# A retention and snake-activation kernel on one core: who casts the first half of batch 2, and when the last state sum of batch 1 is added

## The chip, the cores and the metric

The kernel runs on one core of a Trainium2 chip. A core has TensorE (matrix products into PSUM), VectorE (called DVE in the profile), ScalarE (ACT), GpSimd (POOL), SyncE (SP, here used to issue DMAs) and DMA engines. Each engine takes its instructions in the order in which they stand in its own queue, and waits where a semaphore says so. The metric is the device time of one execution in microseconds (us). Before the change it was 311.66 us, the median of three runs (311.43 to 312.88).

## The reference

For every batch (8), head (8), 576 tokens and head size 64, a masked and decaying attention without softmax is computed, its heads are laid side by side as a row of 512, and a two-layer product with a snake activation follows:

```python
scores = scale * np.matmul(q, k.transpose(0, 1, 3, 2))
gamma = 1.0 - 2.0 ** (-5.0 - np.arange(H, dtype=np.float32))
Dmat = np.where(rel >= 0, gamma[:, None, None] ** rel[None, :, :], 0.0)   # rel = row - column
ret = scores * Dmat[None, :, :, :]
attn_out = np.matmul(ret, v)
x = attn_out.transpose(0, 2, 1, 3).reshape(B * S, H * D)                  # 4608 x 512
h = x @ w_in                                                              # 512 -> 2048
s = np.sin(alpha * h)
g = h + s * s / (alpha + 1e-09)
out = g @ w_out                                                           # 2048 -> 512
```

All inputs and the output are 32-bit floats.

## The kernel before

**Attention.** The first 512 tokens of a batch are done in four chunks of 128, two to a half (p = 0, 1); the last 64 tokens of all batches are gathered into a ninth block. Because the decay is a power of gamma, it can be split into a factor on q and one on k: q and k are loaded as 32-bit numbers and multiplied by those factors (table cn) while being cast to 16 bits. This multiplication is the "cast" of this text: step C, function cast_half (line 203). One cast covers half of the heads of one half p of q or of k, 128 partitions by 512 numbers. On VectorE or GpSimd it is one instruction (line 215); on ScalarE it is eight of 128 x 64 (line 210), as there the factor is a value for each partition. Both casts of k and both of q must be there before the 16 transposes of that half (TR, line 275), which TensorE does for batches 0 to 2 half 0 and DMA transposes (CR, line 232) do for the rest. Then come scores (SP, line 376), mask (SM, line 393), values (VA, line 462) and the part that comes from earlier chunks through a state (ST, line 488); the result is copied to x as 16 bits (XT).

**State.** What chunk c hands on is a sum: kvs[c] = kvs[c-1] times gamma to the 128 (FA, "faded", line 330) plus the product of k and v of chunk c, which stands in PSUM (NS, "next sum", line 334, always on VectorE, since the product is in PSUM). TS (line 346) makes the 16-bit state of it. The three steps of the last chunk of batch 1 are FA 1 2, NS 1 3 and TS 1 3; the last state is used by the ninth block at the end.

**PSUM.** There are three tags: mm (two buffers of two banks each), hp (three banks) and op (one). Transposes, scores, the products of k and v and the values all use mm, and a new tile waits until an older one has been read for the last time.

**The two products.** A block n of 512 tokens is one batch. Its first product (G1, line 584) has 16 units of 128 columns, each with a sine (SI), a square (SQ) and a sum with the product (PR, line 609). The second (G2, line 623) makes 128 rows in four parts and copies them out (OS, with two DMAs on SP each).

**Order.** For batches 0 to 2 the order is written out by hand: TABLE (lines 637 to 977), one step to a line, is followed from top to bottom (lines 1144 to 1150) under a manual schedule, so that each engine gets its instructions in the order in which they stand in the table. The last letter of a step is its engine: V VectorE, A ScalarE, G GpSimd. Loads (LK for q and k on SP, LV for v on GpSimd) stand in the same table. From batch 3 on a loop (line 1158) sets the order. The steps around the change are at lines 829 to 872: the end of batch 1's attention, the second product of block 0, the casts and transposes of batch 2's first half, and the first units of block 1.

Of the kernel before, what the change touches and what calls it, by code (L numbers as in the profile page):

```python
# [16 lines left out]
def kernel(  # L17
# [816 lines left out]
G2 0 1 2 hp  # L834
G2 0 1 3 hp
G2 0 2 3 hp
OS 0 1 A
OS 0 2 A
NS 1 2
# [5 lines left out]
ST 1 1  # L845
XT 1 1 A
OS 0 0 A
C 2 q 0 1 V
C 2 k 0 0 V
G2 0 3 3 hp  # L850
C 2 q 0 0 V
C 2 k 0 1 V
TR 2 0 k
TR 2 0 q
TK 2 0 k A
G1 1 0 hp
SI 1 0
FA 1 2 G
NS 1 3
OS 0 3 V  # L860
TS 1 3 G
C 2 k 1 1 G
# [118 lines left out]
    V, A_, G_ = nc.vector, nc.scalar, nc.gpsimd  # L981

    with tc.manual_schedule():
# [174 lines left out]
        for n in range(2, NBLK):  # L1158
            A = A2
# [104 lines left out]
```

## Time and profile before

| what | value |
|---|---|
| median of three runs | 311.66 us |
| the profiled execution | 311.75 us, span 309.8 us |
| busy share of TensorE, VectorE, ScalarE, GpSimd | 96%, 62%, 73%, 43% |
| a cast of line 215 on VectorE, least and median of the q casts | 0.679 and 0.686 us |
| a cast of line 215 on GpSimd, median of the q casts | 1.050 us |
| one of the 16 instructions of line 210 on ScalarE | 0.333 us |
| a state sum of line 334 | 0.408 to 0.422 us |
| a DMA transpose of k or q, issue to landing | 3.1 to 10.0 us |

The profile shows one execution, traced by instruction. Times in it count from the start of the span; the execution's own time is 1.95 us longer than the span. In a timeline a row gives start, duration, engine, line, operation, output and inputs, and in brackets how long the engine had stood idle and who released it. The chain of waits is followed back from the last instruction: each row is what the next one waited for. A name such as q stands for a raw and for a cast tile alike.

### The profile page before, as it was taken

To read this page: it belongs to the slowest core of one execution; us is meant where nothing else is said; L and a number is where in the kernel's file an instruction comes from. 1 tells how busy PE (TensorE), PEld (TensorE's weight loads), DVE (VectorE), ACT (ScalarE), POOL (GpSimd) and SP (SyncE) were. 2 spreads that over 40 slices of the span, in tenths; PEclk is the share of its full clock that TensorE was granted. 3 is DMA by queue.
4 is the path that set the end of the run, shared out by engine and by line. 5 is a ranking of instruction groups with operands and counts; after the bars stand their busy time and mean duration, and the time that the engine had idled before them with its cause. 6 is when DMAs were issued, how large, how long until landed. Compare 5 with 4: busy or idle time off the path is not lost.

```text
span 309.8 us, 7642 instructions
## 1 busy us (share of the span) xinstructions
PE 296.7 (96%) x3145; PEld 152.7 (49%) x3145; DVE 192.2 (62%) x267; ACT 224.9 (73%) x370; POOL 133.8 (43%) x158
## 2 busy tenths in 40 slices
PE   5799989899899999999999999999999999999995
PEld 5586454444444444544454444544544444444444
DVE  2688957799665356965997699655666343444301
ACT  1469961699588887788778878787787888888810
POOL 3878655669969819901980198209100000000000
PEclk9579999999999999999999999999999999999999
DMA  8999999996999787999999989996331111122133
GB/s 217 210 186 198 262 190 291 180 232 133 152 183 233 157 203 179 118 170 221 170 165 190 178 185 195 164 131 96 70 68 37 35 36 34 34 49 54 34 67 68
DMA packets 118017, 44.74 MB, mean 144 GB/s; under 512 B 84432, under 2 KB 113504, under 8 KB 117984
## 3 DMA queue, kind: packets, MB, share of 16 engines
q1 hardware_dynamic: 83792, 35.08, 55.9%
q0 software_dynamic: 33600, 8.92, 29.7%
q8 instruction: 24, 0.39, 0.6%
q10 hardware_dynamic: 592, 0.28, 0.4%
q14 instruction: 9, 0.07, 0.1%
HBM read 36.91 MB, written 9.44 MB: 150 GB/s over the span
## 4 chain that ended last, share of the span: by engine, by line
PE 80%; DVE 8%; DMA 4%; POOL 3%; ACT 2%; issue 1%; SPq 1%; DVEq 0%; POOLq 0%; ACTq 0%
PE ops L623 37%; PE hps L584 32%; DMA qT<-q 2%; DVE ret L393 2%; DMA k<-in_k_dram 2%; DVE gT L609 2%; PE o L462 2%; PE o L488 2%; PE hps L1065 2%; PE sc L376 1%; PE kv L312 1%; PE ops L1226 1%; PE tr L275 1%; PE sc L407 1%; DVE gT L1092 1%; DVE kvs L334 1%
## 5 line engine op out<-in xcount | busy, mean ns | idle before, releaser
L609 DVE SCALAR_TENSOR_TENSOR gT<-ss_t,inva,hps 128x512 f16<-128x512 f16 x136 | 100.6, 745 | 80.3 <-ACT ss_t L602 79.9
L623 PE MATMUL ops<-w_out,gT 128*128 128x512 f16 x560 | 140.8, 379 | 0.0
L584 PE MATMUL hps<-x,w_in 128*128 128x512 f16 x480 | 120.9, 379 | 1.0 <-DVE gT L609 0.7
L593 ACT ACTIVATE s_t<-hps,alpha_t 128x512 f16<-128x512 f32 x136 | 92.8, 685 | 33.2 <-PE hps L584 32.1
L584 PEld LDWEIGHTS <-w_in 128*128 128x128 f16 x544 | 52.8, 98 | 64.6 <-issue 1.6
L623 PEld LDWEIGHTS <-gT 128*128 128x128 f16 x560 | 53.0, 98 | 60.9 <-DVE gT L609 0.3
L602 ACT ACTIVATE ss_t<-s_t 128x512 f16<-128x512 f16 x127 | 79.9, 631 | 2.6
L346 POOL TENSOR_TENSOR s<-kvs,cn 128x512 f16<-128x512 f32 x28 | 30.2, 1078 | 60.0 <-ACT kvs L319 50.9
L633 ACT COPY osb<-ops 128x512 f32<-128x512 f32 x31 | 18.1, 585 | 13.5 <-PE ops L623 13.1
L126 POOL DMA_DIRECT2D v<-in_v_dram x32 | 22.0, 730 | 0.0
L393 DVE TENSOR_TENSOR ret<-sc,mask 128x1024 f16<-128x1024 f32 x12 | 14.4, 1215 | 6.1 <-PE sc L376 6.1
L215 DVE TENSOR_TENSOR q<-q,cn 128x512 f16<-128x512 f32 x18 | 15.4, 880 | 4.2 <-DMA q<-in_q_dram 4.2
L584 PE MATMUL hps<-x_rest,w_in 128*128 128x512 f16 x64 | 16.4, 379 | 0.0
L432 DVE TENSOR_TENSOR ret<-sc,two 128x1024 f16<-128x1024 f32 x12 | 14.6, 1218 | 0.0
L215 POOL TENSOR_TENSOR q<-q,cn 128x512 f16<-128x512 f32 x14 | 14.6, 1054 | 0.1
L236 ACT CAST x<-o 128x1024 f16<-128x1024 f32 (+1 forms) x13 | 10.8, 851 | 3.7 <-PE o L488 3.4
L604 POOL TENSOR_TENSOR ss_t<-s_t 128x512 f16<-128x512 f16 x10 | 10.4, 1056 | 6.4 <-ACT s_t L593 4.0
L359 POOL TENSOR_TENSOR kvs<-s,kvs 128x256 f32<-128x256 f32 x15 | 11.5, 769 | 1.2
L358 POOL TENSOR_TENSOR s<-kvs,cn 128x256 f32<-128x256 f32 x15 | 11.0, 730 | 0.0
L215 POOL TENSOR_TENSOR k<-k,cn 128x512 f16<-128x512 f32 x9 | 9.9, 1109 | 0.8 <-DMA k<-in_k_dram 0.7
L462 PE MATMUL o<-ret,v 64*64 64x128 f16 (+1 forms) x512 | 10.1, 218 | 0.1
L462 PEld LDWEIGHTS <-v 64*64 64x64 f16 x512 | 7.6, 110 | 4.8 <-issue 4.3
(73 smaller groups left out, 208.1 us busy)
## 6 DMA issues: line engine op xcount, KB each, us to landing
out_dram<-osb SPq DMA_DIRECT2D x70, 128.0 KB, 2.5
q<-in_q_dram SPq DMA_DIRECT2D x14, 512.0 KB, 7.0
k<-in_k_dram SPq DMA_DIRECT2D x32, 128.0 KB, 4.6
k<-in_k_dram SPq DMA_DIRECT2D x7, 512.0 KB, 7.4
q<-in_q_dram SPq DMA_DIRECT2D x8, 256.0 KB, 5.1
v<-in_v_dram POOLq DMA_DIRECT2D x8, 256.0 KB, 5.8
w_in<-in_moe_w_in_dram POOLq DMA_DIRECT2D x4, 512.0 KB, 6.9
w_out<-in_moe_w_out_dram POOLq DMA_DIRECT2D x4, 512.0 KB, 8.3
```

The lines of the kernel that those rows point to most:

```text
L126: nc.gpsimd.dma_start(t_[halves(g), :, s], v[b, :, xs, :].rearrange("h i d -> i h d"))
L215: eng.tensor_tensor(half[b, nm, p][:, :, :, t, :], raw[b, nm, p].rearrange("p (a t) (r d) -> p a t r d", t=2, r=2)[:, :, t], (ct if nm == ...
L346: (eng or nc.gpsimd).tensor_tensor(d_, self.kvs[:, n].unsqueeze(2).to_broadcast([P, 4, 2, D]), g2.unsqueeze(3).to_broadcast([P, 4, 2, D]), ...
L393: nc.vector.tensor_tensor(ret.rearrange("p t (z x) -> p (t z) x", z=2)[:, :, 0:n], sc.rearrange("p t (z x) -> p (t z) x", z=2)[:, :, 0:n], ...
L432: nc.vector.tensor_tensor(ret.rearrange("p t (a x) -> p (t a) x", a=n), sc.rearrange("p t (a x) -> p (t a) x", a=n), m_.unsqueeze(1).to_br ...
L462: nc.tensor.matmul(o[g][halves(t), x0 : x0 + 128].rearrange("p (r i) -> p r i", r=2)[:, :, i0:], x, y, start=(t, g) not in begun, stop=las ...
L584: nc.tensor.matmul(hps, w_in16[:, a, fc * P : (fc + 1) * P], x_of[n][:, a], start=(a == 0), stop=(a == KT - 1),)
L593: nc.scalar.activation(s_t, hps, mybir.ActivationFunctionType.Sin, bias=0.0, scale=alpha_t[:, fc : fc + 1],)
L602: nc.scalar.activation(ss_t, s_t, mybir.ActivationFunctionType.Square)
L609: nc.vector.scalar_tensor_tensor(gT[n][:, fc, :], ss_t, inva[:, fc : fc + 1], hps, MULT, ADD)
L623: nc.tensor.matmul(ops[n, c], gT[n][:, fk, c * P : (c + 1) * P], w_out16[:, fk, :], start=(fk == 0), stop=(fk == FC - 1),)
L633: nc.scalar.copy(osb, ops.pop((n, c)))
```

## The change

Four steps of the table move or change engine; no function is changed. The cast of q's half 1 (C 2 q 0 1) goes from VectorE to ScalarE and stands 11 lines higher, ahead of the output copies OS 0 1 and OS 0 2. VectorE's order of k, q, k casts becomes k, k, then the sum NS 1 3 (with its fade FA 1 2 on GpSimd ahead of it in the table), then the remaining q cast. Before, the fade and the sum stood behind the transposes and the first unit of block 1.

```diff
 G2 0 2 3 hp
+C 2 q 0 1 A
 OS 0 1 A
 OS 0 2 A
 NS 1 2
...
 XT 1 1 A
 OS 0 0 A
-C 2 q 0 1 V
 C 2 k 0 0 V
 G2 0 3 3 hp
+C 2 k 0 1 V
+FA 1 2 G
+NS 1 3
 C 2 q 0 0 V
-C 2 k 0 1 V
 TR 2 0 k
 TR 2 0 q
 TK 2 0 k A
 G1 1 0 hp
 SI 1 0
-FA 1 2 G
-NS 1 3
 OS 0 3 V
 TS 1 3 G
 C 2 k 1 1 G
```

## Prediction

> **What bounds the kernel now.** I read the page first (chain that ended last, busy shares), then the chain from 48 to 62 us, then the orders of VectorE, GpSimd, TensorE and ScalarE there, and last the busy time by stage. The stage table, in which the columns after the stretch are its length, PE, PEld, DVE, ACT, POOL (with instruction counts), clock, DMA share and GB/s:
>
> ```profile
> 54.19:56.99 2.80, 1.83 (x29) 1.10 (x28) 2.80 (x7) 1.69 (x3) 0.00 (x0) 1.00 1.41 249
> ...
> 60.17:71.39 11.22, 10.65 (x182) 5.39 (x172) 11.05 (x17) 10.44 (x19) 8.37 (x10) 1.00 0.97 223
> ...
> 83.01:305.90 222.89, 222.88 (x2136) 108.65 (x2136) 130.82 (x166) 169.69 (x267) 76.16 (x94) 1.00 0.78 123
> ```
>
> From 83.01 us TensorE is busy for 222.88 of 222.89 us at clock 1.00: whatever brings its arrival there forward ends the kernel earlier by as much. The change acts at 54 to 57 us, where VectorE is full, TensorE has a gap and GpSimd stands still. The chain of waits there:
>
> ```profile
> 52.75 1.44 DVE ret L393
> 54.19 0.60 DVE q L215
> 54.80 0.60 DVE k L215
> 55.40 0.60 DVE q L215
> 56.00 0.60 DVE k L215
> 56.60 0.34 DVE kvs L334
> 56.95 0.04 issue
> 56.99 1.05 PE tr L275 x16
> ```
>
> Four casts and the state sum (NS 1 3) stand in line on VectorE, and batch 2's transposes start when the sum ends. TensorE's own order shows the gap, GpSimd's and ScalarE's what they do meanwhile:
>
> ```profile
> 55.06 1.03 PE L623 MATMUL ops<-w_out,gT 128*128 128x512 f16 x4
> 56.99 0.61 PE L275 MATMUL tr<-ident,k 128*128 128x128 f16 x8 [0.91 <-DVE kvs L334]
> 57.43 0.61 PE L275 MATMUL tr<-ident,q 128*128 128x128 f16 x8
> 57.88 1.89 PE L584 MATMUL hps<-x,w_in 128*128 128x512 f16 x8
> ```
> ```profile
> 53.02 0.61 POOL L330 TENSOR_TENSOR s<-kvs,cn 128x256 f32<-128x256 f32 x1
> 57.01 1.04 POOL L346 TENSOR_TENSOR s<-kvs,cn 128x512 f16<-128x512 f32 x1 [3.38 <-DVE kvs L334]
> ```
> ```profile
> 52.93 0.58 ACT L236 COPY osb<-ops 128x512 f32<-128x512 f32 x1 [5.96 <-PE ops L623]
> 53.79 0.58 ACT L236 COPY osb<-ops 128x512 f32<-128x512 f32 x1 [0.28 <-PE ops L623]
> 55.26 1.01 ACT L236 CAST x<-o 128x1024 f16<-128x1024 f32 x1 [0.88 <-PE o L488]
> ```
>
> The reader is to see three things. The first transpose waited for the sum, not only for its data: it writes the PSUM buffer from which the sum reads (two buffers carry the tag mm). ScalarE is idle for 5.96 us before 52.93. The sum's other input was ready at 53.02 + 0.61 = 53.63, long before its turn.
>
> **The change, part by part.**
>
> *A q cast leaves VectorE.* One instruction of 0.68 us, 0.60 from start to start, goes off the chain: all that follows it there can start 0.60 sooner.
>
> *It becomes eight instructions on ScalarE.* The 16 of the same kind (line 210) took 3.91 us in all with 0.333 each, so one every (3.91 - 0.333)/15 = 0.238; eight end 7 x 0.238 + 0.333 = 2.0 us after the first starts. They wait for the load of q, issued at 43.81 and landed 6.7 us later, at 50.5, so they end at about 52.5, inside the idle 5.96 us: cost nothing. Behind them stand OS 0 1, OS 0 2, XT 1 1, OS 0 0 and TK 2 0. OS 0 1 starts at 52.93, so 0.4 us is spare; the two copies (about 0.5 each from start to start) are followed by an idle 0.88, so XT 1 1 at 55.26 moves only if the cast ends after 54.26.
>
> In a sentence of its own: the Trainium skill, ScalarE: Activation LUTs, Rules for kernel authors, gives multiplies to VectorE and budgets some 0.3 us per ACTIVATE plus 0.83 ns per element, by which eight of 64 would take an estimated 2.8 us and end at 53.3; OS 0 1 would slip 0.4 us and the sum would stay, since the trace's 0.238 decides.
>
> *The k casts move up, the sum goes ahead of the last q cast.* VectorE becomes k at 54.12, k at 54.72, sum at 55.32 (ends 55.73 instead of 56.94), q at 55.65, ending 56.33. The first k was cast at 54.72 without a wait and would now be asked for at 54.12; its load, issued at 44.37, landed 8.0 us later, at 52.4, so no wait. The fade (FA 1 2) keeps its place in GpSimd's order, as no other GpSimd step lies between its old and new line, and nothing is issued to a DMA queue by any step moved; the order on SP is unchanged.
>
> *TensorE.* G2 0 3 3 starts at 55.06 and passes the array to the next group 4 x 0.217 later, at 55.93. Then sum (55.73) and k casts (55.40) are done: the k transposes run from 55.93 to 56.37. The q transposes need q at 56.33; between a cast's end and the load of its weights lay 0.06 (56.60 to 56.66), between that and the matmul 0.16 to 0.33, so they start between 56.55 and 56.72, say 56.6, and the next product (G1 1 0) 0.45 later, at 57.05 instead of 57.88: 0.83 us gained (0.71 to 0.88). If the transposes got another mm buffer, the one XT 1 1 empties at 56.27, the k part would start at 56.33 and G1 at 57.2: 0.66. I take 0.83, since the trace names the sum as releaser. G1's input from XT 1 1 (56.27) is there.
>
> *GpSimd.* Its to-state (TS 1 3) is released at 55.80 instead of 57.01, but a q cast with two SBUF inputs is running then. The nearest row is at 49.94: VectorE's 0.69 us (line 346) met a GpSimd fade released at 49.98, and the fade took 1.12 instead of 0.61 while VectorE lost nothing. So TS 1 3 ends 0.47 + (1.04 - 0.61) = 0.9 after the cast, at 57.2 instead of 58.05: 0.8 earlier, in step with TensorE. Its four casts for batch 2's second half, ending at 62.08, and the transposes on SP behind them follow; k and q for them land at 54.5 and 56.2, in time.
>
> *Where the gain goes.* From 60.17 VectorE, TensorE and ScalarE hand each other work (11.05, 10.65 and 10.44 of 11.22 us), so all shift. The last wait before the full stretch is TensorE's 0.82 us at 83.01 for batch 3's q transpose by DMA, issued at 75.84 and landed 7.0 us later; its issue hangs on GpSimd's casts, and these on ScalarE's sines, which shift as well. The only fixed things are loads: if batch 3's stayed where they are, q (64.03 + 5.7 = 69.7) would meet a cast moved from 70.23 to 69.4 and take back 0.3.
>
> Sum: -0.60 (cast away) and -0.60 (sum ahead of the other), cut to -0.83 by the q cast and TensorE's own order; all else 0. The profiled execution took 311.75 us (span 309.8 and 1.95 around it), 0.09 above the median: 311.75 - 0.83 = 310.92, against the median 311.66 - 0.83 = 310.8.
>
> **The rivals.**
>
> *GpSimd takes the port first.* If TS 1 3 starts before the q cast, the cast waits. At 39.57 GpSimd had started and VectorE's cast at 40.13 took 1.07 instead of 0.68, ending 0.56 after GpSimd. Then q ends at 55.80 + 1.04 + 0.56 = 57.4, G1 starts at 58.1: 0.2 slower, 311.9. For it: the two come within 0.15 us. Against: VectorE starts its next instruction 0.07 before the one in front ends, GpSimd 0.07 after it. The Trainium skill, SBUF — State Buffer, Who interferes with whom, says the same: an instruction with two SBUF inputs on VectorE and a reading one on GpSimd block each other whole, and issue order decides who waits; by that rule it is all or nothing, and the two rows agree.
>
> *ScalarE waits for q (slower).* Place: the first of the eight. The load lands at 50.5; the slowest of this line's loads in the profile took 10.8 us, which would be 54.6. Then the cast ends at 56.6, XT 1 1 at 58.6, and G1 starts at 58.65: 0.8 slower, 312.4. It decides once q lands after 53.8; from 53.0 on it eats the gain. Against: all that precedes this load is untouched.
>
> *Eaten downstream.* Batch 3's loads do not move, or another stage has slack that fills: 0.3 to 0.8 lost, 311.1 to 311.7.
>
> *Batch 3's DMA transposes move by themselves.* These landed after 3.1 to 10.0 us in this profile, the deciding one after 7.0, in a stretch with DMA share 1.32. At under 6 us TensorE's wait is gone and the gain grows to 0.83 + 0.98 (82.03, when it was free, to 83.01) = 1.8: 309.85. At 10.0 it costs 3.0 - 0.83 = 2.2: 313.8; over 9.4 it decides beyond the bound below. For it: the order of traffic shifts. Against: the loads, the value load and the transposes all hang on the same shifting engines.
>
> **How the numbers follow.** Forecast (0.5 to 1.1 gained) 0.50; eaten downstream 0.13; port 0.07; q late 0.05; DMA transposes sooner 0.13, later 0.12. About 0.5%, 1.56 us, is what a measurement of this kernel can tell from no change. Only the last two cases pass it, so faster 0.13, same 0.75, slower 0.12; the likeliest case's own range is 310.5 to 311.2. Eight in ten are held by 310.1 to 312.3: this takes in the port, nearly all of a late q, and part of both DMA cases.
>
> **What would show it.** Right: eight line-210 instructions ending before the first output copy; sum ahead of the last q cast; the gap of TensorE before the k transposes gone, a short one (0.2) before q; G1 1 0 at about 57.05; TensorE's full stretch from about 82.2. Wrong: the q cast over 1 us long, ScalarE idle before line 210 past 53 us, or a DMA wait at 83 us other than 0.8.

## The result and the profile after

| | before | changed |
|---|---|---|
| median of 22 runs | 311.92 us | 310.95 us |
| lowest and highest | 310.93 to 312.97 us | 309.72 to 313.06 us |
| ratio to before, 95% interval | | 0.9966 (0.9952 to 0.998) |
| profiled execution | 311.75 us, span 309.8 | 311.88 us, span 309.6 |

The change takes 0.34% off, about 1.06 us of 311.92 (0.62 to 1.50). The two profiled executions happen to lie within 0.2 us of each other, so their spans cannot be set against each other; the distances inside them can. Two are used throughout. **D1** runs from the start of the last products of the second product ahead of batch 2's transposes (line 623) to the start of the first product of block 1 (line 584). **D2** runs from there to batch 3's first scores (line 376), where TensorE's last wait ahead of its full stretch lies. Starting at line 623 leaves out what went on earlier, which moves these products between 54.6 and 56.5 us in the profiles of this study though its code is the same in all of them. What follows D2, from batch 3's first scores to the end of the span, takes 226.7 to 227.1 us in all thirteen profiles (227.1 and 226.7 in the two of the changed kernel): it varies by up to 0.4 us from execution to execution, but not with the change.

The row of before at which D2 ends, which is TensorE's last wait ahead of its full stretch:

```profile
83.01 0.64 PE L376 MATMUL sc<-qT,kT 64*64 64x128 f16 x32 [0.82 <-DMA qT<-q]
```

TensorE's timeline of the changed kernel (start, duration, engine, line, operation, number; in brackets the idle time ahead and its releaser):

```profile
55.60 1.03 PE L623 MATMUL ops<-w_out,gT 128*128 128x512 f16 x4
56.46 0.61 PE L275 MATMUL tr<-ident,k 128*128 128x128 f16 x8
57.03 0.61 PE L275 MATMUL tr<-ident,q 128*128 128x128 f16 x8
57.47 1.89 PE L584 MATMUL hps<-x,w_in 128*128 128x512 f16 x8
...
82.49 0.64 PE L376 MATMUL sc<-qT,kT 64*64 64x128 f16 x32 [0.71 <-DMA qT<-q]
```

D1 is 57.47 - 55.60 = 1.87 us, against 57.88 - 55.06 = 2.82 before: 0.95 gained. The k transposes now follow the products without a wait, and only a small gap (from 56.46 + 0.44 = 56.90 to 57.03; 0.44 is the distance from k to q transposes in the kernel before) is left ahead of the q transposes. D2 is 25.02, against 83.01 - 57.88 = 25.13. Together that is 1.06 us, what the times say. That it agrees to the hundredth is chance: the 0.11 us of D2 lies in the wait for batch 3's DMA transpose (0.71 against 0.82 us), and that wait differs from one profile to the next.

VectorE, GpSimd and ScalarE of the changed kernel:

```profile
54.66 1.28 DVE L215 TENSOR_TENSOR k<-k,cn 128x512 f16<-128x512 f32 x2
55.87 0.41 DVE L334 TENSOR_TENSOR kvs<-s,kv 128x256 f32<-128x256 f32 x1
56.20 0.68 DVE L215 TENSOR_TENSOR q<-q,cn 128x512 f16<-128x512 f32 x1
```
```profile
56.35 1.43 POOL L346 TENSOR_TENSOR s<-kvs,cn 128x512 f16<-128x512 f32 x1 [2.18 <-DVE kvs L334]
```
```profile
50.42 2.02 ACT L210 ACTIVATE q<-q,cn 128x64 f16<-128x64 f32 x8 [2.91 <-DMA q<-in_q_dram]
53.48 0.59 ACT L236 COPY osb<-ops 128x512 f32<-128x512 f32 x1 [1.04 <-PE ops L623]
```

The sum comes third instead of fifth in VectorE's line. GpSimd's to-state step meets the q cast and takes 1.43 us instead of 1.04, while the cast keeps its 0.68. ScalarE's eight instructions lie in what was idle time, with 1.04 us to spare before the first output copy. The margin depends on when the load of q lands: in the other profiles with this one cast on ScalarE (e1, e3, e4, e8, e9 and e10 below) it is between 0.1 us (e8) and 0.9 us (e10), and the copy starts 2.12 to 2.14 us ahead of the products of line 623 in all of them, as in the kernel before (2.13).

The chain of waits of the changed kernel (start, duration, what) no longer runs through the casts:

```profile
53.30 1.45 DVE ret L393
54.75 0.04 issue
54.79 0.42 PE o L462 x16
55.21 0.55 PE o L488 x8
55.76 0.86 PE ops L623 x4
56.63 1.01 PE tr L275 x16
```

From the mask (line 393) it now goes over TensorE's own values, states and products straight to the transposes.

### The profile page after: what moved, and what is told of

Its sections match the earlier page's. It is cut to its first block, busy times and chain, and to the rows that moved or that the text cites. A ratio compares the mean times of both kernels' runs of the same rounds, so it can differ in the third digit from the quotient of the medians.

```text
span 309.6 us, 7650 instructions
## 1 busy us (share of the span) xinstructions
PE 296.6 (96%) x3145; PEld 152.4 (49%) x3145; DVE 192.7 (62%) x266; ACT 227.0 (73%) x378; POOL 134.1 (43%) x158
## 3 DMA queue, kind: packets, MB, share of 16 engines
q1 hardware_dynamic: 83792, 35.08, 56.5%
## 4 chain that ended last, share of the span: by engine, by line
PE 80%; DVE 8%; DMA 4%; POOL 3%; ACT 2%; issue 1%; SPq 1%; DVEq 0%; POOLq 0%; ACTq 0%
PE ops L623 37%; PE hps L584 32%; DVE ret L393 3%; DMA qT<-q 2%; DMA k<-in_k_dram 2%; DVE gT L609 2%; PE o L462 2%; PE o L488 1%; PE tr L275 1%; PE ops L1226 1%; PE kv L312 1%; PE sc L376 1%; DVE kvs L334 1%; POOL s L330 1%; PE sc L407 1%
## 5 line engine op out<-in xcount | busy, mean ns | idle before, releaser
L215 DVE TENSOR_TENSOR q<-q,cn 128x512 f16<-128x512 f32 x17 | 14.7, 889 | 4.3 <-DMA q<-in_q_dram 4.3
```

The lines of the kernel that those rows point to most:

```text
L215: eng.tensor_tensor(half[b, nm, p][:, :, :, t, :], raw[b, nm, p].rearrange("p (a t) (r d) -> p a t r d", t=2, r=2)[:, :, t], (ct if nm == ...
```

## The experiments

Each was compared with the kernel before, on the same chip and in the same rounds. All of them:

| run | D1 | D2 | ratio to before (95%) |
|---|---|---|---|
| before | 2.82 | 25.13 | 1 |
| changed | 1.87 | 25.02 | 0.9966 (0.9952 to 0.998) |
| e1: cast to ScalarE only | 2.22 | 24.30 | 0.9981 (0.9967 to 0.9995) |
| e2: sum ahead only | 2.40 | 25.14 | 0.9985 (0.9966 to 1.0004) |
| e3: last q cast twice | 3.32 | 25.17 | 1.0027 (1.0009 to 1.0045) |
| e4: GpSimd casts k first | 2.71 | 25.16 | 0.9998 (0.9981 to 1.0016) |
| e5: ScalarE's cast twice | 1.87 | 24.85 | 0.9985 (0.9969 to 1.0001) |
| e6: ScalarE's cast three times | 2.92 | 25.65 | 1.005 (1.0031 to 1.0069) |
| e7: both q casts on ScalarE | 1.75 | 25.33 | 0.9991 (0.9971 to 1.0012) |
| e8: changed, load of v later | 1.87 | 24.19 | 0.9953 (0.9937 to 0.9969) |
| e9: changed, once more | 1.87 | 24.95 | 0.9973 (0.9958 to 0.9989) |
| e10: as e8, once more | 1.87 | 24.19 | 0.9949 (0.9929 to 0.997) |
| e11: before, load of v later | 2.82 | 24.23 | 0.9977 (0.9959 to 0.9995) |

D1 and D2 are from one profile each, the ratios from 6 to 22 runs.

### Each half of the change alone

e1, against the kernel before:

```diff
 G2 0 2 3 hp
+C 2 q 0 1 A
 OS 0 1 A
...
 OS 0 0 A
-C 2 q 0 1 V
 C 2 k 0 0 V
```

> Only the q cast moves to ScalarE; VectorE keeps k, q, k, then the state sum. The measure is the distance from the start of the last products of line 623 ahead of batch 2's transposes to the start of the first product of block 1 (line 584): 2.82 us in the profile before, 1.87 after the change. Theory of the line on VectorE (each place in it is worth 0.60 us, and the sum releases the transposes): the sum ends 0.60 sooner, the k transposes start 0.60 sooner and still name the sum as releaser; distance 2.2, time about 0.6 us (0.2%) less than before. Rival, that the place of the sum alone made the gain: distance 2.8 and the time of before. Rival, that the transposes would be released by the copy of x on ScalarE instead: distance about 2.2 too, but with that copy as releaser.

e2, against the kernel before:

```diff
 G2 0 3 3 hp
+C 2 k 0 1 V
+FA 1 2 G
+NS 1 3
 C 2 q 0 0 V
-C 2 k 0 1 V
 TR 2 0 k
...
 SI 1 0
-FA 1 2 G
-NS 1 3
 OS 0 3 V
```

> Only the state sum (and its fade) moves ahead of the last q cast; all four casts stay on VectorE in the order q, k, k, sum, q. Theory of the line: the sum ends 0.60 us sooner, so the k transposes start 0.60 sooner, but the q cast ends 0.33 later than the last cast of before, so the q transposes wait for it (a gap of about 0.4 us between k and q transposes) and the first product of block 1 comes after a distance of about 2.6 instead of 2.82; time 0.2 us less than before. Rival, that the order alone is what pays: distance 1.9 and about 0.9 us less.

TensorE's timeline of e1, then of e2:

```profile
55.22 1.03 PE L623 MATMUL ops<-w_out,gT 128*128 128x512 f16 x4
56.55 0.61 PE L275 MATMUL tr<-ident,k 128*128 128x128 f16 x8 [0.30 <-DVE kvs L334]
...
57.44 1.89 PE L584 MATMUL hps<-x,w_in 128*128 128x512 f16 x8
```
```profile
54.61 1.03 PE L623 MATMUL ops<-w_out,gT 128*128 128x512 f16 x4
55.94 0.61 PE L275 MATMUL tr<-ident,k 128*128 128x128 f16 x8 [0.30 <-DVE kvs L334]
56.55 0.62 PE L275 MATMUL tr<-ident,q 128*128 128x128 f16 x8
57.01 1.89 PE L584 MATMUL hps<-x,w_in 128*128 128x512 f16 x8
```

Either half leaves the sum as releaser and takes the wait for it from 0.91 to 0.30 us: one place in VectorE's line is worth 0.60. e1 shortens D1 by 0.60, as expected. e2 shortens it by 0.42 instead of 0.2: the q cast ended at 55.81 + 0.68 = 56.49, and the q transposes started at 56.55, 0.06 later, where 0.27 had been allowed. In the changed kernel the two halves give 0.95 together, a little less than their sum of 1.02: there the k transposes follow TensorE's own products at once (56.46), and the q transposes come 0.15 after their cast. By the times e1 is 0.59 us faster (0.0019 of 312.03), which is D1's part alone: that its profile shows no wait at batch 3's scores (D2 24.30) is not borne out by them, so this one profile stands for itself there. e2's gain the times leave open, as the interval includes 1.

### Does the rest of VectorE's line count, and who wins against GpSimd?

e3, against the changed kernel:

```diff
 C 2 q 0 0 V
+C 2 q 0 0 V
 TR 2 0 k
```

> The changed kernel with its last q cast on VectorE made twice (the same values written again). Theory: the q transposes hang on the end of that cast, so the distance grows from 1.87 by 0.60 to about 2.5 if both casts run back to back, and the whole kernel by the same 0.6 us, which leaves it 0.3 to 0.5 us under before; GpSimd's to-state step then ends 0.6 later. If GpSimd gets in between the two casts, the second ends about 1.0 later still, the distance is about 3.5 and the kernel some 0.6 slower than before. Rival, that the end of the q cast does not matter: distance 1.9 and the time of the changed kernel.

VectorE's casts of q in e3 between 55.5 and 57.9 us (count, then least, median and greatest duration in ns, first and last start), and GpSimd's step beside them:

```profile
L215 DVE TENSOR_TENSOR q<-q,cn x2: 679/1047/1415, 55.7 to 56.5; 128x512 f16<-128x512 f32 x2
```
```profile
55.90 1.42 POOL L346 TENSOR_TENSOR s<-kvs,cn 128x512 f16<-128x512 f32 x1 [2.17 <-DVE kvs L334]
```

The second expected case came about: the first cast takes 0.679 us, GpSimd gets in, and the second takes 1.415. D1 grows by 1.45 (to 3.32, where about 3.5 was expected), and the ratio of 1.0027 is 0.8 us above before, where 0.6 was expected.

e4, against the changed kernel:

```diff
 FA 1 2 G
+C 2 k 1 1 G
 NS 1 3
...
 TS 1 3 G
-C 2 k 1 1 G
 C 2 k 1 0 G
```

> The changed kernel with GpSimd's cast of half of k (second half of batch 2) put ahead of its to-state step, so that GpSimd works while VectorE casts k. Theory that an instruction with two SBUF inputs on VectorE and one on GpSimd exclude each other: GpSimd starts when its k has landed, about 54.5 us; VectorE's k cast or casts beside it take 1.1 to 1.7 us instead of 0.68, the k transposes start 0.4 to 0.9 later, distance 2.3 to 2.8, and the gain of the change is mostly gone. Rival, that they share: VectorE's casts stay at 0.68 to 0.8, distance 1.9.

VectorE's and GpSimd's timelines in e4:

```profile
54.94 2.13 DVE L215 TENSOR_TENSOR k<-k,cn 128x512 f16<-128x512 f32 x2
```
```profile
54.70 1.23 POOL L215 TENSOR_TENSOR k<-k,cn 128x512 f16<-128x512 f32 x1 [0.24 <-PE ops L623]
```

GpSimd started 0.24 us ahead, and VectorE's two casts took 2.13 us instead of 1.28. D1 is 2.71 and the gain is gone (0.9998). So the exclusion that the rival of GpSimd coming first rests on is real; the changed kernel escapes it because the q cast starts first (56.20 against 56.35). That lead of 0.15 to 0.16 us is the same in all nine profiles in which the sum stands right ahead of the q cast on VectorE. The Trainium skill says in SBUF — State Buffer, Who interferes with whom, that issue order decides which of the two is blocked: e3 and e4 show both orders, and agree. The blocked one does not lose quite all of the overlap, though: in the changed kernel GpSimd could start at 56.35, the cast ran to 56.88, and of these 0.53 us GpSimd lost 0.39 (1.43 - 1.04). How much of that difference is only the way durations are recorded is not shown: VectorE's casts in a row overlap by 0.08 us in their own records (0.68 long, 0.60 apart).

### How much room ScalarE has

e5 has ScalarE's step twice, e6 three times, against the changed kernel:

```diff
 C 2 q 0 1 A
+C 2 q 0 1 A
 OS 0 1 A
```

> The changed kernel with ScalarE's q cast made twice (the same values written again), so 1.9 us more on ScalarE. Theory that ScalarE has room there: the casts end 3.9 us after q has landed, about 54.4 us; the first two output copies start up to 1.4 later than before, the copy of x (about 55.3 to 55.8) moves by 0.3 at most, the distance from the last products of line 623 to the first of block 1 stays within 0.1 of 1.87, and the time is that of the changed kernel. Rival, that the cast on ScalarE sits on the path already: distance 2.3 or more and 0.5 us or more slower than the changed kernel.

> The same with the cast made three times, 3.8 us more on ScalarE. Theory of the slack worked out in the prediction: the casts end about 56.2, the copy of x starts about 57.2 instead of 55.3 to 55.8 and ends about 58.2, and the first product of block 1, which reads x, starts about 58.3: distance 2.7 to 3.2 and the whole kernel 0.8 to 1.3 us slower than the changed one, about as fast as the one before or slower. Rival, that ScalarE has more room than that: distance 1.9 and no loss.

ScalarE in e5, with the copy of x in the last row:

```profile
51.45 3.93 ACT L210 ACTIVATE q<-q,cn 128x64 f16<-128x64 f32 x16 [3.14 <-DMA q<-in_q_dram]
55.28 1.04 ACT L236 COPY osb<-ops 128x512 f32<-128x512 f32 x2
56.60 1.01 ACT L236 CAST x<-o 128x1024 f16<-128x1024 f32 x1 [0.27 <-PE o L488]
```

TensorE in e6:

```profile
59.41 0.81 PE L584 MATMUL hps<-x,w_in 128*128 128x512 f16 x3 [0.90 <-ACT x L236]
```

The copy of x has the room that was worked out: twice the cast leaves it waiting for TensorE still (0.27 us) and D1 at 1.87; three times makes TensorE wait 0.90 for x, and D1 is 2.92, inside the expected 2.7 to 3.2. The times do not follow D1 alone. e6 is 1.005, 1.56 us above before, when D1 is only 0.10 above; against the changed kernel the ratios differ by 2.6 us, where 0.8 to 1.3 was expected. What was overlooked stands in the waits of e6 from 60 to 84 us (who waited for what, total, times, longest), and in SP's timeline:

```profile
PE o L488 <- POOL s L346: 1.5, 1, 1.5
...
POOL k L215 <- DMA k<-in_k_dram: 1.2, 1, 1.2
...
POOL q L215 <- DMA q<-in_q_dram: 0.6, 1, 0.6
```
```profile
58.00 6.50 SPq L1034 DMA_DIRECT2D out_dram<-osb  x8
...
67.41 0.58 SPq L151 DMA_DIRECT2D k<-in_k_dram  x1
```

The late output copies hold up their DMAs on SP (58.00, against 54.09 in the changed kernel), behind which stand batch 2's DMA transposes and then batch 3's loads (first one 67.41, against 63.38). GpSimd's casts of batch 3 then wait for their data, the state that GpSimd makes behind them (line 346) is late, TensorE waits 1.5 us for it at line 488, a wait that the changed kernel does not have, and D2 grows by 0.6 over the changed kernel's; the wait for batch 3's transposes is gone in exchange. D1 and D2 together make e6 0.62 us slower than before; the interval of the time begins at 0.97, and what makes up the rest this profile does not show. In e5 the first copy is 1.0 us late, counted from the products of line 623, and GpSimd waits 0.4 us for q, but TensorE does not wait for the state, and D2 (24.85) is no longer than the changed kernel's. e5's time of 0.9985 lies between the two kernels; its interval overlaps that of the changed kernel and reaches 1, so whether the second cast costs anything the times leave open.

e7, against the changed kernel:

```diff
 C 2 q 0 1 A
+C 2 q 0 0 A
 OS 0 1 A
...
-C 2 q 0 0 V
 TR 2 0 k
```

> Both q casts of the half go to ScalarE, none is left on VectorE (k, k, sum). Theory: ScalarE's sixteen instructions end about 54.4, still ahead of the copy of x; the q transposes follow the k transposes without the gap of 0.13, the distance becomes 1.75 instead of 1.87; GpSimd's to-state step runs unhindered (1.04 instead of 1.43 us). Time 0.1 us less than the changed kernel, too little to see in the times. Rival, that ScalarE's later output copies and copy of x hold up TensorE: distance 2.2 or more, slower than the changed kernel.

TensorE in e7 up to block 1, and waits from 60 to 84 us:

```profile
55.56 1.03 PE L623 MATMUL ops<-w_out,gT 128*128 128x512 f16 x4
56.42 0.61 PE L275 MATMUL tr<-ident,k 128*128 128x128 f16 x8
56.87 0.61 PE L275 MATMUL tr<-ident,q 128*128 128x128 f16 x8
57.31 1.89 PE L584 MATMUL hps<-x,w_in 128*128 128x512 f16 x8
```
```profile
PE o L488 <- POOL s L346: 0.7, 1, 0.7
POOL q L215 <- DMA q<-in_q_dram: 0.7, 1, 0.7
...
POOL k L215 <- DMA k<-in_k_dram: 0.3, 1, 0.3
```

D1 is 1.75, to the hundredth as expected, with no gap left between TensorE's own pieces, and GpSimd's step took 1.05 us with no q cast beside it. Yet the output copies came 1.2 us later (54.71, against 53.48), SP's queue with them (batch 3's first load at 64.48), GpSimd waited for k and q, TensorE waited 0.7 us for GpSimd's state as in e6, and D2 grew by 0.31. The expected 0.1 us is lost again; whether e7 is slower than the changed kernel the intervals leave open.

### The wait at the end of the stage

e8, against the changed kernel; e10 is the same kernel once more, e9 the changed kernel once more in e10's rounds, and e11 the kernel before with this edit alone:

```diff
 CR 3 0
-LV 3 1
 C 3 q 1 1 G
...
 LV 3 0
+LV 3 1
 TS 2 3 G
```

> The changed kernel with one load of v for batch 3 (its second half) issued behind batch 3's last q cast and the other load of v instead of right beside the DMA transposes of batch 3's first half. Theory that this load competes with the transposes: they land within about 5 us instead of 6.9 to 7.4, TensorE's wait of 0.7 us for them (about 82 us) is gone, the distance from the first product of block 1 (57.47) to batch 3's first scores (82.49) shrinks from 25.0 to 24.2, and the kernel is about 0.8 us faster than the changed one, ratio to before about 0.994. Rival, that the transposes are slow in themselves: they still land after 6 to 7 us and the time is that of the changed kernel.

> The changed kernel once more, to stand beside the next two in the same rounds. Expected: ratio to before 0.9966 within 0.0015; distance from the last products of line 623 to the first of block 1 1.87 us; batch 3's first scores 25.0 later, with a wait of 0.5 to 0.9 us for the DMA transposes.

> The changed kernel with the load of v for batch 3 moved behind the last q cast, once more. Theory that the wait for the DMA transposes is real time: distance to batch 3's first scores 24.2 without a wait, and 0.4 to 0.9 us less than the changed kernel in the same rounds, ratio to before 0.994 to 0.9955. Rival, that the time comes back later: the distance is 24.2, but the time is that of the changed kernel within 0.2 us.

> The kernel before with only that load of v moved. If the two gains lie one behind the other on the same path: distances 2.82 and about 24.3, no wait for the transposes, 0.5 to 0.9 us less than before (ratio about 0.9975). Rival, that the load's place pays only together with the change: time of before within 0.2 us.

TensorE in e8, and the landing of the two DMA transposes of batch 3's first half, first in e9, then in e8 (least, median and greatest of the two):

```profile
81.37 1.03 PE L584 MATMUL hps<-x,w_in 128*128 128x512 f16 x4
82.33 0.64 PE L376 MATMUL sc<-qT,kT 64*64 64x128 f16 x32
```
```profile
DMA to landing us min/median/max: 6.9/7.1/7.3
```
```profile
DMA to landing us min/median/max: 3.2/4.1/5.0
```

The wait is gone and D2 is 24.19 in both e8 and e10, 24.23 in e11. The q transpose of batch 3's first half landed 5.0 and 4.9 us after its issue in e8 and e10, against 6.9 in e9; the k transpose after 3.2, against 7.3. In the changed kernel's profile the k transpose landed after 7.4, the landing of the q one is not recorded, and the product that waited for it started 7.07 us after its issue (82.49 - 75.42), against 7.00 in e9. The transposes were issued at the same distance from block 1's first product with and without the load beside them (17.95 and 17.96 us for q, in the changed kernel and e8). In time: e8's ratio is 0.9953, where about 0.994 was expected; e10 is 0.65 us under e9 in the same rounds (310.56 against 311.21), e11 1.05 under before by the medians and 0.7 by the ratio. By D1 and D2 the two gains lie one behind the other, and the kernel of e8 and e10 has the lowest ratios of the study, 0.9953 and 0.9949. That it beats the changed kernel rests on D2 and on the medians of e9 and e10; the intervals of the ratios overlap.

## Why the prediction was right

**The sign, the place and the size** were right: forecast 310.8 us for a 0.83 us gain, measured 310.95 and 1.06 (0.62 to 1.50). That the time itself came within 0.15 us is partly luck: the forecast started from 311.66, which is 0.26 below the median of the 22 runs before, and its gain was 0.23 too small, two errors that offset each other. The forecast's own pieces:

- *VectorE's line.* Two places of 0.60 us were to be won, one by the cast that leaves and one by the sum that goes ahead. e1 and e2 show each by itself at 0.60 to 0.61 of the wait for the sum.
- *What caps it.* TensorE's products were to pass the array on 0.87 us after their start, and did after 0.86 (55.60 to 56.46). The remaining wait for the q cast was sized too large: 0.27 from the cast's end to the first q transpose (56.33 to 56.6), where 0.15 (after) and 0.06 (e2) were measured. That is the 0.12 by which D1 came out better than the 0.83. Its upper figure, 0.33 from the load of weights to the matmul, was no such distance: in that row (56.66 to 56.99) the matmul waited for the state sum.
- *ScalarE at no cost.* 2.0 us was forecast, 2.02 measured, ended 1.04 ahead of the first copy where 0.4 was forecast; how much is left depends on when the load of q lands. (The Trainium skill's budget in ScalarE: Activation LUTs, Rules for kernel authors, gave an estimated 2.8; the row of before was the better guide.) The margin for the copy of x was right, as e5 and e6 show from both sides. What the step left out is SP's queue behind the output copies: it had said that SP's order does not change, and had not asked what a late copy does to that order. In the changed kernel the copies are not late, so it cost nothing here; in e6 and e7 it did.
- *GpSimd's step.* It was to end 0.9 us after the q cast; it ended 56.35 + 1.43 - 56.88 = 0.90 after. That VectorE would win hung on 0.15 us, but not on luck, as the same lead in all nine profiles shows.
- *Downstream.* That all shifts together held: D2 is 25.02 and 24.95 in the changed kernel, 25.13 before, and most of the difference lies in the wait for the DMA transpose. The loads that might have eaten 0.3 did not.
- *The DMA transposes.* The rival let them land by themselves anywhere from 3.1 to 10.0 us. Eight of the nine profiles with the load of v beside them, e6 left out, show a wait of 0.5 to 0.9 us; only e1's has none. (In e6 TensorE comes there too late to wait.) Most of it is the load's doing, as e8, e10 and e11 show. The rival's price for the good side (0.98) was near the 0.8 to 0.9 by which D2 shrank.

The gain lies within the half per cent that was named as what a measurement can tell; with 22 runs of each kernel the interval became narrower than that and lies below 1, so it is a small gain and not none.

## What to carry to other kernels

When several producers stand in line on one engine, read off which one of them releases the next engine, and put that one first; it may be a reader of a buffer and not the maker of the data. Before moving work into another engine's idle time, follow not only what that engine must do next but the DMA queue behind it: here outputs, transposes and the next loads shared SP's queue, and 1.2 us of lateness in a copy (e7) came out as 0.3 us at the far end, while 1.0 us (e5) did not show there. And look at the last wait before the bottleneck runs full: moving one load away from the transfers that TensorE waits for took 0.8 to 0.9 us off D2, and alone (e11) 0.7 us off the time by the ratio, against 1.06 for the change itself.

## What the runs showed of the hardware that was not expected

With a load of 256 KB issued by GpSimd beside them, two DMA transposes landed 5.9 to 7.6 us (first) and 5.5 to 7.1 us (second) after their issue, in the profiles that record the landing; without it 3.2 and 4.9 to 5.0. Two instructions on VectorE and GpSimd that exclude each other cost the blocked one less than the whole overlap: GpSimd's step ended 0.90 us after the cast although it takes 1.04 alone, though part of this difference may lie in how durations are recorded. And between two casts of VectorE that stand back to back, a waiting GpSimd step gets its turn (e3), so that repeating a 0.60 us cast cost 1.45.
